# Layer-norm sums folded to 64 rows and stacked with their rounding rest, and the same for the last 64 tokens of a product with U

## The chip, the cores and the metric

The kernel runs on one core of a Trainium2 chip. The metric is device time in microseconds of one launch, the median of three runs. The profile is one further execution, taken by the hardware profiler; its times are counted from the first instruction of the span.

## What is computed

Three layers, batch 8, 576 tokens, 512 channels, all in fp32 with fp32-like accuracy:

```python
# 1: attention over keys and values pooled by 8 (72 of them), 8 heads of 64
attn = softmax(q @ k_p.T / 8);  x = (attn @ v_p) as [8, 576, 512]
# 2: token mixing of rank 32, then an MLP with residual
h = x.transpose(0, 2, 1) @ U @ V          # U [576, 32], V [32, 576]
u = x + h.transpose(0, 2, 1)
x = u + np.maximum(u @ w_ch1, 0.0) @ w_ch2
# 3: layer norm over the 512 channels, then an MLP with residual
mu  = np.mean(x, axis=-1, keepdims=True)
var = np.mean((x - mu) ** 2, axis=-1, keepdims=True)
xn  = (x - mu) / np.sqrt(var + 1e-06) * g_ln
out = x + np.maximum(xn @ w_ch1, 0.0) @ w_ch2
```

## The kernel before

Most products are made in fp32r, a rounded fp32 format in which TensorE takes one pass. To keep the accuracy, an operand is split into a rounded part (`h`, made on ScalarE or VectorE) and the rest (`l`, the difference, on VectorE or GpSimd), and a product is the sum of three: high by high, high by low, low by high. The function `split` (L547) makes both parts.

The program doesn't write an order by hand. Each step is an `Order.op` (L107) with the engines that it may run on and an estimated cost for each, the buffers that it reads and writes, and a priority that follows TensorE's estimated time. `schedule` (L151) is a list scheduler over TensorE, ScalarE (ACT), VectorE (DVE), GpSimd (POOL) and the SyncE queue (SP, all transfers): it plays the estimates through, and what it places on an engine is that engine's instruction order. Each engine then works strictly in that order and waits at an instruction whose inputs aren't there. A transfer is estimated at 1.3 us, plus its bytes at 250 per ns in one queue, plus 1.0 us.

There are two stages. The first (up to some 600 us) is attention by batch and head pair, interleaved with the first half of the MLP of layer 2 (`a_l1` L1279, `a_l2` L1306). For batches 2 to 7, `att_xt` (L991) transposes the attention output of a batch into five tiles of 128 tokens by 512 channels and splits each into `xh` and `xl`; `att_g` (L1008) multiplies both with the stationary tile `ust[:, i]` and sums all in one PSUM bank. The 576 tokens give four whole tiles; the fifth starts at token 448, so its rows 0 to 63 repeat tokens of the fourth, and the rows of U for them are zeros: `setup_uv` (L637) clears that half of the raw tile and loads the last 64 rows of U into the other. Batches 0 and 1 go another way (`tm_g`, L1075) with the fp32 copy `us` of U.

The second stage is three passes over nine groups of 512 tokens (`passes`, L1769): the second half of layer 2's MLP, then the two halves of layer 3's. A group is four units (`unit` L1505 and `second` L1593); a unit is seven blocks of six 256-column products (L1520) and eight of three 512-column products (L1608). Blocks sum into PSUM banks of the rings `pa` and `pbc` (two each); copies `s` (L403 or L405) take a bank's state away before the next block is added to it. `group_prep` (L1462) loads a group's tokens into `xraw` and makes split operands `op` for the next group: the rounded part on ScalarE, the rest on GpSimd (L556).

The layer norm of a group (`norm`, L1695) runs beside the next group of pass 0, and for the last group beside the first of pass 1. It has four steps, spread over the units. `n0` adds the four channel blocks on GpSimd into `lns`. `n1` splits `lns` into `lnh` and `lnl`, takes two products with `ones` (128 by 128, each element 1/512), which give the mean in every row of a `pbc` bank, subtracts it from the four blocks on VectorE and stores the result to `n_d`. `n2` squares the four blocks on ScalarE and adds them on GpSimd. `n3` makes the variance with four fp32 products in which `lns` is the stationary tile and the moving operand is one column (L1743), so that the 512 tokens come out as 128 rows by 4; then a square root, a reciprocal and one Newton step on small tiles, and a transfer `r_d` of 512 numbers to DRAM. The reciprocal root is used only in pass 2, where it is read back (L1675).

Of the kernel before, what the change touches and what calls it, by code (L numbers as in the profile page):

```python
# [20 lines left out]
DM = 512  # L21
# [400 lines left out]
class Kern:  # L422
    def __init__(self, nc, tc, aps):
# [68 lines left out]
        for a in ("lnh", "lnl"):  # L492
            ring(b2, a, [128, TG], F32R)
# [12 lines left out]
    def setup(self, ctx):  # L506
# [7 lines left out]
        self.minus = cp.tile([128, 128], F32R, tag="minus", name="minus")  # L514
        nc.scalar.mul(self.minus, self.ident, -1.0)
        few = cp.tile([128, 2], F32, tag="few", name="few")
        self.eps, self.mean = few[:, 0:1], few[:, 1:2]
        nc.gpsimd.memset(self.eps, 1e-6)
        nc.gpsimd.memset(self.mean, 1.0 / DM)
# [10 lines left out]
        self.p_d = [dp.tile([128, NCC, TG], F32, tag=f"p_d{g}", name=f"p_d{g}") for g in range(NG)]  # L530
        self.r_d = [dp.tile([1, TG], F32, tag=f"r_d{g}", name=f"r_d{g}") for g in range(NG)]
# [28 lines left out]

    def split_ps(self, hi, lo, ps, src, n, m):

        nc, o = self.nc, self.o
        on = {ACT: c_act(n, True), DVE: c_dve(n)}
        part = lambda: src(ps.t)
        o.op({ACT: on[ACT]}, lambda e: copy(nc, e, hi(), part()), r=[ps], w=[hi.a])
        o.op(
            {PE: c_pe(n)},
            lambda e: e.matmul(part(), self.minus[:m, :m], hi(), start=False, stop=True, skip_group_check=True),
            r=[hi.a],  # L570
            w=[ps],
        )
        o.op(on, lambda e: copy(nc, e, lo(), part()), r=[ps], w=[lo.a])
# [63 lines left out]
    def setup_uv(self):  # L637
# [4 lines left out]
        def load(raw):  # L642
            o.op(
                {GP: 200},
                lambda e: e.memset(raw.t[:64, 4 * RANK : n].bitcast(I32), 0),
                w=[raw],
            )
            o.op(
                {SY: 450},
                lambda e: e.dma_start(  # L650
                    raw.t[:, : 4 * RANK].rearrange("p (i r) -> p i r", r=RANK),
                    self.U[:512].rearrange("(i p) r -> p i r", p=128),
                ),
                w=[(raw, 0)],
                size=131072,
            )
            o.op({SY: 450}, lambda e: e.dma_start(raw.t[64:, 4 * RANK : n], self.U[512:]), w=[(raw, 1)], size=16384)
# [333 lines left out]
    def att_xt(self, b, i):  # L991
        o = self.o
        ps, xh, xl = self.buf("py"), self.buf("xh"), self.buf("xl")
# [8 lines left out]
        if NP * b < LEAN_X:  # L1002
            self.split_ps(View(xh, None, whole), View(xl, None, whole), ps, whole, DM, 128)
        else:
            self.split(View(xh, None, whole), View(xl, None, whole), View(ps, None, whole), DM, ps=True, hi_on=(ACT,))
        self.xhl[i] = (xh, xl)

    def att_g(self, b, i):  # L1008
# [9 lines left out]
        self.o.op({PE: c_pe(DM, 2)}, mm, r=[xh, xl, self.ust], w=[pg])  # L1018
# [676 lines left out]
    def norm(self, g):  # L1695
# [9 lines left out]
        nt = TG // 128  # L1705
# [7 lines left out]

        def n1():
            hi, lo, ps, s = self.buf("lnh"), self.buf("lnl"), self.buf("pbc"), b["s"]
            whole = lambda t: t
# [21 lines left out]
        def n3():  # L1738
            s, ps, sd, ve = b["s"], self.buf("pbc"), self.buf("lnd"), self.buf("lnv")

            def mm(e):
                for i in range(nt):
                    e.matmul(  # L1743
                        ps.t[:, i : i + 1], s.t[:, i * 128 : i * 128 + 128], self.mean, start=True, stop=True,
                        skip_group_check=True,
                    )

            o.op({PE: nt * 240}, mm, r=[s], w=[ps], full=True)
            part = lambda: ps.t[:, :nt]
            small = {DVE: 70}  # L1750
            o.op({ACT: 150}, lambda e: e.activation(sd.t, part(), AF.Sqrt, bias=self.eps), r=[ps], w=[sd])
            o.op({DVE: 130}, lambda e: e.tensor_scalar_add(ve.t, part(), 1e-6), r=[ps], w=[ve])
# [82 lines left out]
LEAN_X = 8  # L1835
# [51 lines left out]
```

## Time and profile before

| | |
|---|---|
| Time, median of 3 runs | 1762.2 us (1757.46 to 1763.09) |
| The profiled execution's own time | 1756.1 us |
| Its span, first to last instruction | 1754.3 us |
| TensorE busy | 1729.4 us (99%) |
| VectorE, ScalarE, GpSimd busy | 959.6, 714.5, 753.9 us (55%, 41%, 43%) |
| TensorE's granted clock, mean | 0.999 |
| Traffic | 222.99 MB, mean 127 GB/s |

Busy time is the union of an engine's instructions; TensorE's products overlap in the records, since they are pipelined, so the distance from start to start tells what one costs. PE is TensorE, PEld its weight loads, DVE VectorE, POOL GpSimd, SP the queue that issues transfers.

### The profile page before, as it was taken

How to read it: one execution, taken by the hardware profiler on the slowest of the kernel's cores; microseconds unless marked ns; L12 is line 12 of the kernel's file. 1: busy time of each engine (PE TensorE's matmuls, PEld its weight loads, DVE VectorE, ACT ScalarE, POOL GpSimd, SP SyncE). 2: the span in 40 equal slices, each digit the busy share in tenths (PEclk: the TensorE clock that was granted, in tenths of full speed). 3: DMA queues.
4: the chain of work that ended last, by engine and by line, in shares of the span. 5: the costliest groups of instructions: out<-in, count | busy, mean ns of one | idle time of the engine just before them, and what ended most of it. 6: DMA issues, size and time to landing. Idle time of an engine off the chain costs nothing.

```text
span 1754.3 us, 27128 instructions
## 1 busy us (share of the span) xinstructions
PE 1729.4 (99%) x10302; PEld 1525.7 (87%) x10302; DVE 959.6 (55%) x1839; ACT 714.5 (41%) x1812; POOL 753.9 (43%) x655
## 2 busy tenths in 40 slices
PE   6999999999999999999999999999999999999998
PEld 6888888888888899999999889999999999999997
DVE  7998887888655344444445756553225633333333
ACT  5765655655522233333333443333333332223221
POOL 3442312311100166666667643333335455555554
PEclk9999999999999999999999999999999999999999
DMA  6665554555143334444443453431112422333322
GB/s 201 217 201 170 184 182 147 179 174 162 55 165 108 130 111 121 121 121 121 120 121 115 126 163 125 134 121 67 49 49 85 144 103 103 110 119 103 103 79 78
DMA packets 96691, 222.99 MB, mean 127 GB/s; under 512 B 15408, under 2 KB 15792, under 8 KB 90800
## 3 DMA queue, kind: packets, MB, share of 16 engines
q1 hardware_dynamic: 96416, 221.26, 39.9%
q8 instruction: 80, 1.31, 0.3%
q14 instruction: 51, 0.42, 0.1%
q10 hardware_dynamic: 144, 0.00, 0.0%
HBM read 151.85 MB, written 69.37 MB: 126 GB/s over the span
## 4 chain that ended last, share of the span: by engine, by line
PE 91%; DVE 2%; DMA 1%; POOL 0%; issue 0%; ACT 0%; DVEq 0%; POOLq 0%; ACTq 0%
PE py L1608 33%; PE pa L1520 17%; PE pbc L1520 13%; PE pbc L1319 11%; PE pa L1291 11%; PE py L398 2%; PE py L847 2%; PE py L978 1%; PE py L979 1%; PE py L1016 0%; PE py L1015 0%; DVE w1l L556 0%; PE py L1185 0%; PE pbc L1743 0%; DMA wraw<-w_d 0%
## 5 line engine op out<-in xcount | busy, mean ns | idle before, releaser
L1608 PE MATMUL py<-hid,w2h 128*128 128x512 f32 x1728 | 541.2, 394 | 0.2 <-DVE hid L1548 0.2
L1608 PE MATMUL py<-hid,w2l 128*128 128x512 f32 x864 | 338.7, 392 | 0.0
L1520 PE MATMUL pa<-op,w1h 128*128 128x256 f32 x1728 | 326.2, 281 | 1.4 <-DVE s L405 1.0
L1520 PEld LDWEIGHTS pa<-op,w1h 128*128 128x128 f32 x1728 | 293.8, 188 | 37.9 <-DVE s L405 1.5
L556 POOL TENSOR_TENSOR op<-xraw,op 128x512 fp32r<-128x512 f32 x130 | 171.9, 1324 | 276.9 <-ACT op L403 272.0
L1578 DVE TENSOR_TENSOR pbc<-s,pbc 128x512 f32<-128x512 f32 x108 | 75.2, 696 | 382.2 <-PE pbc L1520 382.2
L1608 PEld LDWEIGHTS py<-hid,w2h 128*128 128x128 f32 x1728 | 273.7, 189 | 11.1 <-DVE hid L1548 0.5
L1520 PEld LDWEIGHTS pbc<-op,w1h 128*128 128x128 f32 x1296 | 220.8, 188 | 28.1
L1520 PE MATMUL pbc<-op,w1h 128*128 128x256 f32 x1296 | 244.3, 281 | 0.0
L1520 PE MATMUL pa<-op,w1l 128*128 128x256 f32 x864 | 242.7, 281 | 0.0
L1608 PEld LDWEIGHTS py<-hid,w2l 128*128 128x128 f32 x864 | 162.5, 188 | 36.7
L1319 PE MATMUL pbc<-op,wh 128*128 128x512 f32 x576 | 182.1, 397 | 0.0
L1520 PE MATMUL pbc<-op,w1l 128*128 128x256 f32 x648 | 181.8, 281 | 0.0
L1291 PE MATMUL pa<-hid,wh 128*128 128x512 f32 x576 | 180.5, 394 | 0.0
L1520 PEld LDWEIGHTS pa<-op,w1l 128*128 128x128 f32 x864 | 163.0, 189 | 0.0
L1548 DVE SCALAR_TENSOR_TENSOR hid<-pa,hid 128x512 fp32r<-128x512 f32 x108 | 74.5, 690 | 125.1 <-ACT hid L1542 124.8
L1542 ACT ACTIVATE hid<-pa 128x512 fp32r<-128x512 f32 x108 | 64.6, 598 | 190.8 <-PE pa L1520 180.9
L1542 ACT ACTIVATE hid<-pbc 128x512 fp32r<-128x512 f32 x108 | 64.6, 598 | 180.4 <-DVE pbc L1578 179.5
L1474 POOL TENSOR_TENSOR t<-xraw 128x512 f32<-128x512 f32 x52 | 67.4, 1296 | 141.3 <-DMA xraw<-n_d 89.4
L1291 PEld LDWEIGHTS pa<-hid,wh 128*128 128x128 f32 x576 | 105.8, 188 | 21.3 <-DVE op L1298 0.2
L1520 PEld LDWEIGHTS pbc<-op,w1l 128*128 128x128 f32 x648 | 121.9, 188 | 0.0
L1319 PEld LDWEIGHTS pbc<-op,wh 128*128 128x128 f32 x576 | 103.8, 188 | 19.4
(210 smaller groups left out, 2864.2 us busy)
## 6 DMA issues: line engine op xcount, KB each, us to landing
xraw<-n_d SPq DMA_DIRECT2D x18, 1024.0 KB
wraw<-wC SPq DMA_DIRECT2D x32, 512.0 KB
wraw<-wA SPq DMA_DIRECT2D x24, 512.0 KB
w_d<-wx SPq DMA_DIRECT2D x48, 256.0 KB
wraw<-w_d SPq DMA_DIRECT2D x48, 256.0 KB
k<-kT SPq DMA_DIRECT2D x32, 288.0 KB
q<-qT SPq DMA_DIRECT2D x32, 288.0 KB
v<-v SPq DMA_DIRECT2D x32, 288.0 KB
```

The lines of the kernel that those rows point to most:

```text
L398: e.matmul(out, src, ident, start=first, stop=True, is_transpose=True, skip_group_check=True)
L556: lambda e: e.tensor_sub(lo(), src(), hi().bitcast(F32)),
L847: lambda e: e.matmul(ps.t[:, i : i + 2 * SP], q.t[:, QT[t] : QT[t] + 128], kbd.t.rearrange("p h n -> p (h n)"), start=True, stop=True, ski ...
L978: e.matmul(ps.t[:, :SH], w, eh.t[:, h, c], start=True, stop=False)
L1291: e.matmul(ps.t, w.t[:, c], u.t, start=(i == 0), stop=(i == 3 * NCC - 1))
L1319: e.matmul(ps.t, w.t[:, c], x.t, start=(f == 0 and j == 0), stop=(f == NA - 1 and j == 2))
L1474: o.op(on, lambda e: e.tensor_sub(dst(), a(), c()), r=r, w=w)
L1520: e.matmul(bank.t[:, sl], w.t[:, self.WCOL[k], c], u.t[:, t], start=(first and i == 0), stop=(last and i == 5), skip_group_check=True,)
L1542: lambda e: e.activation(h.t[:, :TG], bank.t, AF.Relu),
L1548: lambda e: e.scalar_tensor_tensor(l.t[:, :TG], bank.t, 0.0, h.t[:, :TG].bitcast(F32), op0=ALU.max, op1=ALU.subtract),
L1578: o.op({DVE: c_dve(TG)}, lambda e: e.tensor_add(c.t, s.t, c.t), r=[s], w=[c])
L1608: e.matmul(y.t, w.t[:, i, c], x.t[:, :TG], start=(first and q == 0), stop=(last and q == 2))
```

## The change

The sum over channels needs only to add up 128 rows. The new `mean()` first adds the upper 64 rows of the sum to the lower 64 (a copy to `lnq` on ScalarE, an addition on GpSimd), rounds the 64 rows into the lower half of `lnh` (ScalarE) and puts the rest into its upper half (GpSimd). One product with `ones` then sums rounded part and rest together. `n1` and `n3` both use it. In `n3` the variance now lies along the columns of one row; it is copied from PSUM to `lnq`, written to a DRAM row `s_d` and read back as 128 rows by 4, from where the square root goes on as before.

In `att_xt` the fifth tile keeps only its 64 new tokens: the rounded part in rows 64 to 127, the rest in rows 0 to 63 of the same tile, with the last 64 rows of U loaded into both halves, so `att_g` makes one product of it instead of two. For `us` the lower half is cleared after the copies.

The tiles `lnl` and `minus`, the constant `mean` and the function `split_ps` go. The core of the diff:

```diff
@@ setup
-        self.minus = cp.tile([128, 128], F32R, tag="minus", name="minus")
-        nc.scalar.mul(self.minus, self.ident, -1.0)
@@ setup_uv
-            o.op({GP: 200}, lambda e: e.memset(raw.t[:64, 4 * RANK : n].bitcast(I32), 0), w=[raw])
...
-            o.op({SY: 450}, lambda e: e.dma_start(raw.t[64:, 4 * RANK : n], self.U[512:]), w=[(raw, 1)], size=16384)
+            for z in range(2):
+                r = slice(64 * z, 64 * z + 64)
+                o.op(
+                    {SY: 450},
+                    lambda e, r=r: e.dma_start(raw.t[r, 4 * RANK : n], self.U[512:]),
+                    w=[(raw, 1 + z)],
+                    size=16384,
+                )
...
+        o.op({GP: 200}, lambda e: e.memset(self.us.t[:64, 4], 0.0), w=[self.us])
@@ att_xt
-        if NP * b < LEAN_X:
-            self.split_ps(View(xh, None, whole), View(xl, None, whole), ps, whole, DM, 128)
+        if i < 4:
+            self.split(View(xh, None, whole), View(xl, None, whole), View(ps, None, whole), DM, ps=True, hi_on=(ACT,))
         else:
-            self.split(View(xh, None, whole), View(xl, None, whole), View(ps, None, whole), DM, ps=True, hi_on=(ACT,))
+            o.op({ACT: c_act(DM, True)}, lambda e: copy(nc, e, xh.t[64:], ps.t[64:]), r=[ps], w=[(xh, 1)])
+            o.op(
+                {DVE: c_dve(DM)},
+                lambda e: e.tensor_sub(xh.t[:64], ps.t[64:], xh.t[64:].bitcast(F32)),
+                r=[ps, (xh, 1)],
+                w=[(xh, 0)],
+            )
@@ att_g
-            e.matmul(pg.t, self.ust.t[:, i], xh.t, start=(i == 0), stop=False)
-            e.matmul(pg.t, self.ust.t[:, i], xl.t, start=False, stop=(i == 4))
+            e.matmul(pg.t, self.ust.t[:, i], xh.t, start=(i == 0), stop=(i == 4))
+            if i < 4:
+                e.matmul(pg.t, self.ust.t[:, i], xl.t, start=False, stop=False)
@@ norm
+        def mean():
+            s, q, h, ps = b["s"], self.buf("lnq"), self.buf("lnh"), self.buf("pbc")
+            on = {ACT: c_act(TG)}
+            o.op(on, lambda e: e.copy(q.t[:64], s.t[64:]), r=[s], w=[q])
+            o.op(eng, lambda e: e.tensor_add(s.t[:64], s.t[:64], q.t[:64]), r=[q], w=[s])
+            o.op(on, lambda e: e.copy(h.t[:64], s.t[:64]), r=[s], w=[(h, 0)])
+            o.op(
+                eng,
+                lambda e: e.tensor_sub(h.t[64:], s.t[:64], h.t[:64].bitcast(F32)),
+                r=[s, (h, 0)],
+                w=[(h, 1)],
+            )
+            o.op({PE: c_pe(TG)}, lambda e: e.matmul(ps.t, self.ones, h.t, start=True, stop=True), r=[h], w=[ps])
+            return ps
...
         def n1():
-            hi, lo, ps, s = self.buf("lnh"), self.buf("lnl"), self.buf("pbc"), b["s"]
-            self.split(View(hi, None, whole), View(lo, None, whole), View(s, None, whole), TG, hi_on=(ACT,), lo_on=(GP,))
-            def mm(e):
-                e.matmul(ps.t, self.ones, hi.t, start=True, stop=False)
-                e.matmul(ps.t, self.ones, lo.t, start=False, stop=True)
-            o.op({PE: c_pe(TG, 2)}, mm, r=[hi, lo], w=[ps])
+            ps = mean()
...
         def n3():
-                for i in range(nt):
-                    e.matmul(
-                        ps.t[:, i : i + 1], s.t[:, i * 128 : i * 128 + 128], self.mean, start=True, stop=True,
-                        skip_group_check=True,
-                    )
-            o.op({PE: nt * 240}, mm, r=[s], w=[ps], full=True)
+            ps, row, sd, ve = mean(), self.buf("lnq"), self.buf("lnd"), self.buf("lnv")
+            v = Buf(None)
+            o.op({ACT: c_act(TG, True)}, lambda e: e.copy(row.t[:1], ps.t[:1]), r=[ps], w=[row])
+            o.op({SY: 450}, lambda e: e.dma_start(self.s_d[g], row.t[:1]), r=[row], w=[v], size=2048)
+            o.op(
+                {SY: 450},
+                lambda e: e.dma_start(ve.t, self.s_d[g].rearrange("o (i p) -> p (o i)", p=128)),
+                r=[v],
+                w=[ve],
+                size=32768,
+            )
+            o.op({ACT: 150}, lambda e: e.activation(sd.t, ve.t, AF.Sqrt, bias=self.eps), r=[ve], w=[sd])
+            o.op({DVE: 70}, lambda e: e.tensor_scalar_add(ve.t, ve.t, 1e-6), w=[ve])
```

## Rows read from the trace of the kernel before

**Rows 1.** The page: busy time of the engines, and granted clock in 40 slices.
```profile
PE 1729.4 (99%) x10302; PEld 1525.7 (87%) x10302; DVE 959.6 (55%) x1839; ACT 714.5 (41%) x1812; POOL 753.9 (43%) x655
...
PEclk9999999999999999999999999999999999999999
```
**Rows 2.** Busy time of each engine by stretch: start, attention, pass 0.
```profile
core 0: us, PE busy (x) PEld busy (x) DVE busy (x) ACT busy (x) POOL busy (x), PEclk, DMA share, GB/s
0.00:44.00 44.00, 30.49 (x185) 27.07 (x186) 31.86 (x87) 23.47 (x75) 16.42 (x38) 1.00 0.68 202
...
352.00:416.00 64.00, 64.00 (x343) 54.15 (x342) 54.18 (x117) 40.04 (x144) 13.58 (x17) 1.00 0.49 160
731.00:774.00 43.00, 43.00 (x274) 38.86 (x273) 18.44 (x33) 15.37 (x30) 27.56 (x23) 1.00 0.45 124
```
**Rows 3.** Waits of TensorE: for whom, us in total, times, longest.
```profile
PE py L847 <- DMA q<-qT: 5.3, 1, 5.3
PE py L847 <- issue: 3.8, 1, 3.8
...
PE pa L1520 <- DVE s L405: 1.0, 1, 1.0
```
**Rows 4.** The chain that ended last: start, us, what; two groups each of passes 0, 1.
```profile
643.86 1.38 PE py L1608 x6
...
687.27 1.38 PE py L1608 x6
...
1036.24 1.38 PE py L1608 x6
...
1078.31 1.39 PE py L1608 x6
```
**Rows 5.** TensorE in order of time: start, us, line, what, count.
```profile
230.45 0.39 PE L1015 MATMUL py<-xh,ust 128*128 128x512 f32 x1
...
230.91 0.63 PE L1291 MATMUL pa<-hid,wh 128*128 128x512 f32 x2
...
657.02 0.40 PE L1720 MATMUL pbc<-lnh,ones 128*128 128x512 f32 x1
...
657.49 0.39 PE L1520 MATMUL pa<-op,w1h 128*128 128x256 f32 x2
...
678.47 0.95 PE L1743 MATMUL pbc<-few,lns 128*128 128x1 f32 x8
679.28 0.49 PE L1520 MATMUL pa<-op,w1h 128*128 128x256 f32 x2
679.60 0.28 PE L1520 MATMUL pa<-op,w1l 128*128 128x256 f32 x1
...
680.76 0.40 PE L1520 MATMUL pbc<-op,w1h 128*128 128x256 f32 x2
...
682.18 0.40 PE L1520 MATMUL pa<-op,w1h 128*128 128x256 f32 x2
```
**Rows 6.** A group of instructions: busy us, mean ns of one, idle before and its releaser.
```profile
L403 ACT CAST lnh<-lns 128x512 fp32r<-128x512 f32 x9 | 5.6, 622 | 10.6 <-POOL lns L1712 10.6
```
**Rows 7.** GpSimd in order of time, in the same group.
```profile
652.53 1.31 POOL L556 TENSOR_TENSOR lnl<-lns,lnh 128x512 fp32r<-128x512 f32 x1
...
664.22 1.29 POOL L1736 TENSOR_TENSOR lns<-lns,lnq 128x512 f32<-128x512 f32 x1 [0.74 <-ACT lnq L1735]
669.62 1.30 POOL L556 TENSOR_TENSOR op<-xraw,op 128x512 fp32r<-128x512 f32 x1 [4.11 <-ACT op L403]
```
**Rows 8.** ScalarE in order of time, behind the norm's products.
```profile
680.27 0.37 ACT L403 COPY s<-pa 128x256 f32<-128x256 f32 x1
```
**Rows 9.** The transfers' queue and the first reader of `xraw`, in order of time.
```profile
678.89 0.52 SPq L1484 DMA_DIRECT2D xraw<-u_d  x1
...
683.24 0.57 SPq L1761 DMA_DIRECT2D r_d<-lnd  x1
...
683.84 0.62 ACT L403 CAST op<-xraw 128x512 fp32r<-128x512 f32 x1 [0.39 <-DMA xraw<-u_d]
```

More of the change, by code (lines that the diff above doesn't have):

```diff
@@ L491, in __init__ @@
         ring(b2, "yt", [128, NCC, TG])
-        for a in ("lnh", "lnl"):
-            ring(b2, a, [128, TG], F32R)
+        ring(b2, "lnh", [128, TG], F32R)
         for a in ("lns", "lnq"):
@@ L513, in setup @@
         nc.gpsimd.memset(self.ones.bitcast(F32), 1.0 / DM)
-        self.minus = cp.tile([128, 128], F32R, tag="minus", name="minus")
-        nc.scalar.mul(self.minus, self.ident, -1.0)
-        few = cp.tile([128, 2], F32, tag="few", name="few")
-        self.eps, self.mean = few[:, 0:1], few[:, 1:2]
+        few = cp.tile([128, 1], F32, tag="few", name="few")
+        self.eps = few[:, 0:1]
         nc.gpsimd.memset(self.eps, 1e-6)
-        nc.gpsimd.memset(self.mean, 1.0 / DM)
         self.neg_b = cp.tile([128, 1], F32, tag="negb", name="neg_b")
@@ L530, in setup @@
         self.p_d = [dp.tile([128, NCC, TG], F32, tag=f"p_d{g}", name=f"p_d{g}") for g in range(NG)]
+        self.s_d = [dp.tile([1, TG], F32, tag=f"s_d{g}", name=f"s_d{g}") for g in range(NG)]
         self.r_d = [dp.tile([1, TG], F32, tag=f"r_d{g}", name=f"r_d{g}") for g in range(NG)]
@@ L559, in split @@
         )
[L561 to L571, printed above, removed]
-        )
-        o.op(on, lambda e: copy(nc, e, lo(), part()), r=[ps], w=[lo.a])
     def decode(self, x, tmp, raw):
@@ L643, in load @@
             o.op(
[L644 to L648, printed above, removed]
                 {SY: 450},
@@ L991, in att_xt @@
     def att_xt(self, b, i):
-        o = self.o
-        ps, xh, xl = self.buf("py"), self.buf("xh"), self.buf("xl")
+        nc, o = self.nc, self.o
+        ps, xh, xl = self.buf("py"), self.buf("xh"), self.buf("xl") if i < 4 else None
         xs = [self.xT[NP * b + p] for p in range(NP)]
@@ L1014, in mm @@
         def mm(e):
-            e.matmul(pg.t, self.ust.t[:, i], xh.t, start=(i == 0), stop=False)
-            e.matmul(pg.t, self.ust.t[:, i], xl.t, start=False, stop=(i == 4))
-        self.o.op({PE: c_pe(DM, 2)}, mm, r=[xh, xl, self.ust], w=[pg])
+            e.matmul(pg.t, self.ust.t[:, i], xh.t, start=(i == 0), stop=(i == 4))
+            if i < 4:
+                e.matmul(pg.t, self.ust.t[:, i], xl.t, start=False, stop=False)
+        r = [xh, xl, self.ust] if i < 4 else [xh, self.ust]
+        self.o.op({PE: c_pe(DM, 2 if i < 4 else 1)}, mm, r=r, w=[pg])
     def tm_v(self, P, z):
@@ L1704, in norm @@
         b = {}
-        nt = TG // 128
         eng = {GP: c_pool(TG)}
@@ L1712, in n0 @@
             o.op(eng, lambda e: e.tensor_add(s.t, s.t, q.t), r=[q], w=[s])
-        def n1():
-            hi, lo, ps, s = self.buf("lnh"), self.buf("lnl"), self.buf("pbc"), b["s"]
-            whole = lambda t: t
-            self.split(View(hi, None, whole), View(lo, None, whole), View(s, None, whole), TG, hi_on=(ACT,), lo_on=(GP,))
-            def mm(e):
-                e.matmul(ps.t, self.ones, hi.t, start=True, stop=False)
-                e.matmul(ps.t, self.ones, lo.t, start=False, stop=True)
-            o.op({PE: c_pe(TG, 2)}, mm, r=[hi, lo], w=[ps])
+        def mean():
[12 more added lines that the diff above has]
+            return ps
+        def n1():
+            ps = mean()
             for c in range(NCC):
@@ L1834 @@
 LEAN_T = 8
-LEAN_X = 8
 W_LEAD = (-12000.0, 8000.0)
```

6 lines of the change are left out of this document (removed).

## Prediction

> **What bounds the kernel now.** I read the page first: TensorE is busy for 99% of the span and its clock stands at the upper of its two levels, 2.4 GHz, in every slice [rows 1]. A busy TensorE can still be a waiting one, since the ends of its products are modelled, so I then took stretches: 30.49 of the first 44 us, but no idle time at all later, 64.00 of 64 in the attention stage and 43.00 of 43 in pass 0 [rows 2]. The list of its waits says the same: the long ones are at the start (5.3 us for the first load, 3.8 us of issue), and of the passes only 1.0 us behind a copy `s` is listed among them [rows 3]. Last, the period, from the chain of work: the same place of a 512-token group comes after 687.27 - 643.86 = 43.41 us in pass 0 and after 1078.31 - 1036.24 = 42.07 us in pass 1 [rows 4]. Both groups have the same products but for the norm, so the norm costs TensorE 1.34 us per group, and nothing else holds it. Hence behind the start each product taken off TensorE is worth its spacing, as long as the other engines keep up.
>
> **The norm's products.** In `n1` the two products with `ones` start at 657.02 and the next ones at 657.49 [rows 5]: 0.47 us, so one is 0.235 us. In `n3` the eight records of the four fp32 products begin at 678.47 and the next product at 679.28: 0.81 us. The pair of 256-column products behind them takes 679.60 - 679.28 = 0.32 us; a pair has as many columns as one product of 512, 0.235, so 0.085 us of turning from fp32 goes too: 0.895 us [rows 5]. The two together, 1.365 us, agree with the 1.34 of the periods. The change leaves one product of 0.235 us in each: n1 saves 0.235, n3 saves 0.895 - 0.235 = 0.66, together 0.895 us per group; nine groups: 8.05 us. I take the row's 0.235 for the new product since it has the same stationary tile and 512 columns; it has no lower price than that of its own shape, and rows give no reason for a higher one.
>
> A page of the Trainium skill would price it otherwise. TensorE: Matmul & The Clock Gate, Back-to-back issue gap, gives about 131 ns per 512-column product in a sustained stream; the spacing here is 235 ns, so the trace disagrees, and by the page the whole gain would be about 8.9 us (an estimate from that figure) instead of the sum below.
>
> **The product with U.** `att_xt` runs for six batches (2 to 7). Both halves of one token tile start at 230.45 and the next product at 230.91: 0.46 us, one is 0.23 [rows 5]. Six fifth tiles lose one each: 1.4 us. TensorE is full there, 64.00 of 64 us [rows 2], so it counts whole. If VectorE (54.18 of 64) were the true limit, it would be nothing; its subtraction and ScalarE's rounding stay as they are in number. The copy across partitions has no row on VectorE; below nothing is excluded, since no element is dropped from its 512, and twice its time would still be beside a full TensorE.
>
> **What is added, and what covers it.** POOL gets three operations per group (one in n1, two in n3). The nearest row is the subtraction `lnl`, 1.31 us at 128 rows [rows 7]; with half of the rows the free size is the same, so I take 1.3 us each, 3.9 per group, between nothing and twice that for writing to other partitions than it reads. POOL is busy 27.56 of 43 us in pass 0 [rows 2]: 31.5 of 42.5 then, 35.4 at the dear end. What could be late is a split for the next group. The sums of squares end at 664.22 + 1.29 = 665.5 and the first split of the next group starts at 669.62 [rows 7]; the second fold's chain (copy 0.62, add 1.3, copy 0.62, subtraction 1.3, some 4 us) fits that gap nearly, and a split pushed back is made at 670.9 and used at 680.76 [rows 5, 7]: almost 10 us of cover. Without that cover each microsecond would be one of TensorE. The first fold delays n1's product by a copy and an addition, 1.9 us; `lnl` was ready at 652.53 + 1.31 = 653.84 and its product ran at 657.02 [rows 5, 7], 3.2 us of cover.
>
> ScalarE gets four passes more per group (three copies at `lnh`'s 622 ns [rows 6] and the row from PSUM, about 0.6): 2.5 us on 15.37 of 43 [rows 2]. They stand in a queue in which the `s` copies wait, which TensorE needs. The copy at 680.27 ends at 680.64 and its bank is written again at 682.18 [rows 5, 8]: 1.5 us of cover for each. A copy of 0.6 us goes under it.
>
> n3 now sends 512 numbers to DRAM and back before the square root. SP gets both issues: the second waits for the first to land, and behind it are the `yt` load and the `x_d` stores. The whole of `xraw`, issued at 678.89, was used at 683.84, 4.95 us later [rows 9]; a small transfer behind it lands about then. One round is therefore between 0.57 us (an issue alone [rows 9]) and 4.95 us; I take 4.95 for both, as bulk loads lie in front. The result `r_d` is read in pass 2, hundreds of microseconds later, so the 10 us cost nothing as long as no engine stands for them. The `pbc` bank is held from the product to the row copy, about as long as today to the square root and addition.
>
> **Start and constants.** The cleared half of the raw tile becomes a second 16 KB load on SP, and `us` is cleared in 64 rows after its copies; `minus` goes, a ScalarE operation made while TensorE waits 5.3 us for its first load [rows 3]. Zero, with the first load as cover; an SP issue in front of the next loads could cost its 0.57 [rows 9]; the clearing makes POOL wait for three copies of `us`, and behind it stand only additions of `v` for later heads. The removed `split_ps` branch belongs to batches 0 and 1, which don't call `att_xt`: nothing.
>
> **Order.** The list scheduler places everything anew from its own costs, which can move the waits where TensorE is not full: 44 - 30.5 = 13.5 us in the first 44 [rows 2]. I bound a shift by the largest wait that order could make or remove there, 3.8 us of issue [rows 3], either way, and take zero.
>
> **Sum.** 8.05 + 1.4 = 9.4 us. The profiled execution took 1756.1 us, so 1746.7 on its own scale. The median of the three runs is 1762.2, 6 us above it, and the three spread over 5.6 us; the same work off the median gives 1752.8 us.
>
> **Rivals.** First, the slower side: **ScalarE stands for the round trip.** The square root waits for `ve` in an in-order queue, with the `s` copies and the Relus behind it. If the order puts it before the data land, say one round of 4.95 us early, TensorE loses 4.95 - 1.5 = 3.45 us per group, nine times 31 us, less 9.4: 1784 us. It decides from a stand of 1.5 + 0.9 + 0.16 = about 2.5 us per group, where cover and gain are used up. For it: two dependent transfers behind 1 MB loads, and an order fixed beforehand. Against: the scheduler's figures for 1 MB (1.3 us, 4.2 us at 250 bytes per ns, 1.0 us: 6.5) are longer than the 4.95 measured [rows 9], so it puts the root late rather than early. The Trainium skill (DMA: Bandwidth & Descriptors, Anatomy of one DMA) gives about 2.0 us fixed for one transfer issued from GpSimd, and an estimate from it is 4 us for the two transfers of the round; no row here shows one by itself.
>
> Second, **the new order eats half of the gain**: 3.8 us more waiting at the start or at the change of pass and 0.2 us of ScalarE's queue in each of nine groups, 5.6 us: 1762.2 - 9.4 + 5.6 = 1758.4 us. For it: the first 44 us depend on a chain, not on TensorE. Against: the changed loads there are small.
>
> Third, **the order also gains**: a wait of 3.8 us goes, 1749.0 us.
>
> That the change doesn't do what it says would be a POOL that cannot keep up: 35.4 of 42.5 us at the dear end is still below, and the splits have 10 us. I give it no chance of its own; it would look like the first rival.
>
> **How the numbers follow.** A comparison of this kernel can tell about 0.3%, 5.3 us, from no change. Forecast 0.68, gaining order 0.05: faster 0.73. Half eaten: 0.16, within. Standing ScalarE: 0.11, slower. The time is the forecast's, 1752.8. The range leaves the first rival out. Downward it takes the 3.8 us and the 5 us by which runs of one kernel lie apart, 1744; upward it reaches the second rival and the same scatter, 1763.
>
> **What would show it.** Period of pass 0: 42.5 us, between 43.4 and pass 1's unchanged 42.06. Eighteen products with `ones`, no fp32 product with `few`, 24 instead of 30 products with the low half in the product with U. POOL near 31 us per group, and no wait of TensorE for `s` or a split over 1 us. The attention period 0.23 us shorter. It is wrong if the period stays near 43.4 or more with TensorE waiting for an `s` copy behind a ScalarE that waits for `ve`, or if the first 44 us come out some microseconds longer.

## The result, and the profile after

Six runs of each kernel beside each other: before 1762.6 us (1757.5 to 1767.4), after 1784.5 us (1780.0 to 1789.8). The ratio is 1.0124, 95% interval 1.0103 to 1.0145: the change makes the kernel 22 us slower, where 9.4 us less had been forecast. The profiled execution of after took 1784.5 us (span 1782.7), its median. That of before took 1756.1, 6 us less than its median, so differences between the two traces come out some microseconds larger than the medians; verdicts below go by medians, and traces say where.

The page of after, busy time and granted clock (answers to [rows 1]):

```profile
PE 1737.6 (97%) x10224; PEld 1527.5 (86%) x10224; DVE 967.7 (54%) x1842; ACT 736.5 (41%) x1861; POOL 777.2 (44%) x658
...
PEclk8999999999999999999999999999999999999999
```

TensorE issues fewer products (10224 records, before 10302) and yet is busy for 8 us longer: some of them ran slowly. In 40 slices this can hardly be seen. The waits of TensorE, as in [rows 3], show more:

```profile
PE pbc L1514 <- DVE res L1725: 6.4, 1, 6.4
PE pa L1514 <- ACT s L403: 5.8, 2, 5.4
PE py L833 <- DVE kbd L412: 5.2, 1, 5.2
PE py L833 <- POOL us L658: 3.7, 1, 3.7
PE pa L1514 <- DVE pa L1578: 3.2, 1, 3.2
PE pbc L1514 <- DVE hid L1542: 2.6, 1, 2.6
```

The two of line 833 are those of the start, in size those of before (5.3 and 3.8). The four of line 1514 are new in this size (in before the longest there is 1.0); all but 0.4 us of them lie between 940 and 1110 us, where the kernel goes from pass 0 to pass 1. Now the chain of work (start, us, what), two groups of pass 0 and two of pass 1, as in [rows 4]:

```profile
708.61 1.39 PE py L1602 x6
...
751.15 1.39 PE py L1602 x6
...
1201.20 1.39 PE py L1602 x6
...
1243.27 1.39 PE py L1602 x6
```

The period of pass 0 is 751.15 - 708.61 = 42.54 us, forecast 42.5; pass 1 is unchanged at 42.07. The norm's saving is there, group by group. The loss is elsewhere. To find it, I took the same TensorE product in both traces and subtracted its start in before from that in the other kernel, at seven products (named by their start in before). A difference that grows from one column to the next is time lost between them. The kernels of the experiments stand in the same table.

| kernel | 77 | 183 | 439 | 615 | 961 | 1070 | 1722 us | median less median of before |
|---|---|---|---|---|---|---|---|---|
| after | -1.7 | 6.7 | 11.8 | 11.7 | 5.3 | 28.2 | 28.3 | +21.9 |
| U part alone | -3.5 | 4.6 | 14.9 | 15.1 | 15.1 | 16.1 | 16.1 | +7.8 |
| norm part alone | 2.5 | 2.2 | 2.9 | 3.3 | -3.1 | 19.2 | 19.3 | +12.6 |
| U part, old order | 1.4 | 1.4 | 2.9 | 2.9 | 2.9 | 3.3 | 3.3 | -0.3 |
| after, roots as one run | 1.1 | 8.5 | 15.6 | 15.6 | 9.3 | 13.4 | 13.4 | +1.7 |
| after, roots two issues later | 0.5 | 8.9 | 15.3 | 15.3 | 8.9 | 15.7 | 15.7 | +10.6 |
| norm alone, old order, root on a row | 3.3 | 4.2 | 6.5 | 7.0 | 7.4 | 18.9 | 20.4 | +11.5 |
| norm alone, pieces of 16 bytes | 3.6 | 3.4 | 4.7 | 5.1 | -1.2 | -0.8 | -0.8 | -7.2 |
| after, pieces of 16 bytes | -3.7 | 7.5 | 12.5 | 12.5 | 6.2 | 7.2 | 7.2 | +2.8 |
| the setup of the U part alone | 0.4 | 11.9 | 14.7 | 14.7 | 14.7 | 16.1 | 16.1 | +1.2 |
| the fifth tile alone | 4.1 | 4.6 | 9.5 | 9.6 | 9.6 | 10.4 | 10.4 | +2.1 |

After loses some 13 us in the attention stage (77 to 439), wins 6.4 in pass 0 up to 961, and loses 23 us at the change of pass (961 to 1070). Behind that nothing moves. So there are two losses in two places. In each the clock falls as well. Busy times by stretch (PE, PEld, DVE, ACT, POOL, then granted clock, DMA share, GB/s, as in [rows 2]) in after:

```profile
975.00:980.00 5.00, 4.86 (x17) 4.38 (x18) 1.00 (x1) 2.40 (x6) 3.00 (x3) 0.50 0.49 174
...
1036.00:1041.00 5.00, 1.63 (x7) 1.63 (x8) 4.25 (x8) 1.93 (x4) 2.10 (x2) 0.50 0.50 180
121.00:127.00 6.00, 5.58 (x15) 4.22 (x16) 5.40 (x9) 5.38 (x23) 2.77 (x4) 0.50 0.10 38
```

0.50 is the lower level, 1.2 GHz; in before no slice of the page shows it [rows 1]. It comes right after stretches in which TensorE stood (for 5.4 and 6.4 us; at 121 us after two waits of 1.0), so a wait is paid for again in slow products.

What made TensorE stand at the change of pass is read upward from there: the chain names a transfer, and the SyncE queue says what lies ahead of it. First the chain, then that queue in order of time, then ScalarE's wait, all of after:

```profile
961.91 12.21 DMA wraw<-w_d
...
1024.97 10.30 DMA wraw<-w_d
...
1072.94 8.43 DMA wraw<-wC
```

```profile
946.30 0.24 SPq L1743 DMA_DIRECT2D s_d<-lnq  x1
950.56 0.37 SPq L1746 DMA_DIRECT2D lnv<-s_d  x1
953.40 3.81 SPq L1634 DMA_DIRECT2D x_d<-res  x4
960.93 0.37 SPq L1761 DMA_DIRECT2D r_d<-lnd  x1
961.40 0.93 SPq L1412 DMA_DIRECT2D wraw<-w_d  x2
...
1023.95 0.37 SPq L1761 DMA_DIRECT2D r_d<-lnd  x1
1024.49 0.85 SPq L1412 DMA_DIRECT2D wraw<-w_d  x2
...
1069.83 0.37 SPq L1761 DMA_DIRECT2D r_d<-lnd  x1
1072.94 0.33 SPq L724 DMA_DIRECT2D wraw<-wC  x1
```

```profile
973.49 1.32 ACT L403 CAST w2h<-wraw 128x512 fp32r<-128x512 f32 x2 [6.87 <-DMA wraw<-w_d]
974.72 0.37 ACT L403 COPY s<-pa 128x256 f32<-128x256 f32 x1
```

ScalarE stands 6.87 us for weights of the next pass. The copy `s` behind it comes late, and TensorE waits 5.4 us for that copy. The two loads were issued at 961.40 and landed only 12 us later. Directly ahead of them stands `r_d`, the reciprocal roots, which go out as 512 writes of 4 bytes each. The same at 1024 (10.30 us, then the wait of 6.4) and, with the next load of weights, at 1070 (8.43 us, then the wait of 3.2). The fourth wait, 2.6 us for `hid` at 1000 us, is not of this kind: the kernels below without the small writes have waits of 1.6 to 2.1 us at that place. In before these writes stood elsewhere: ahead of stores that nobody waits for, the weights only behind these.

```profile
943.57 0.37 SPq L1761 DMA_DIRECT2D r_d<-lnd  x1
947.84 3.81 SPq L1640 DMA_DIRECT2D x_d<-res  x4
952.11 9.84 SPq L1418 DMA_DIRECT2D wraw<-w_d  x3
```

What moves during after's wait (first `r_d`'s writes, then two stretches in which the two weight loads should be under way, then the rest of them):

```profile
961.00:963.00 2.00, 2.00 (x13) 1.76 (x12) 0.65 (x2) 0.58 (x1) 2.00 (x2) 1.00 0.13 1
963.00:965.00 2.00, 2.00 (x13) 1.76 (x12) 1.37 (x3) 0.64 (x2) 1.92 (x2) 1.00 0.00 0
965.00:972.00 7.00, 4.73 (x30) 3.90 (x28) 4.24 (x7) 0.60 (x1) 2.94 (x3) 1.00 0.30 17
972.00:974.00 2.00, 0.00 (x0) 0.00 (x0) 0.00 (x0) 0.51 (x1) 0.00 (x0) 0.98 0.96 354
```

The small writes are moved by 963; for 2 us nothing moves at all, for 7 us the loads move at 17 GB/s, then, at once, the queue moves 354. Nothing else is issued behind the loads until 969.76, when a store of 1 MB (`n_d`) follows, which has its part in the 354. This gave the theory that the experiments test: the round trip through DRAM puts the small writes of the roots late, right in front of urgent loads, and the small writes make what follows slow. The rivals: the new order of the list as such; the round trip itself, for which an engine stands (the first rival of the prediction); and that the two parts of the change do each other harm.

### The profile page after: what moved, and what is told of

The parts are those of the page before. It is cut to its first block, busy times and chain, and to the rows that moved or that the text cites. A ratio compares the mean times of both kernels' runs of the same rounds, so it can differ in the third digit from the quotient of the medians.

```text
span 1782.7 us, 27080 instructions
## 1 busy us (share of the span) xinstructions
PE 1737.6 (97%) x10224; PEld 1527.5 (86%) x10224; DVE 967.7 (54%) x1842; ACT 736.5 (41%) x1861; POOL 777.2 (44%) x658
## 4 chain that ended last, share of the span: by engine, by line
PE 80%; DVE 6%; DMA 5%; issue 1%; ACT 0%; SPq 0%; POOL 0%; DVEq 0%; ACTq 0%
PE py L1602 32%; PE pa L1514 16%; PE pbc L1514 12%; PE pa L1285 8%; PE pbc L1313 8%; DMA wraw<-wC 2%; DMA wraw<-w_d 2%; PE py L398 1%; PE py L833 1%; DMA v<-v 1%; DVE xT L972 1%; DMA wraw<-wA 1%; DVE wx L596 0%; DVE wx L604 0%; DVE hid L553 0%
## 5 line engine op out<-in xcount | busy, mean ns | idle before, releaser
L1602 PEld LDWEIGHTS py<-hid,w2h 128*128 128x128 f32 x1728 | 275.5, 190 | 11.7 <-DVE hid L1542 0.5
```

The lines of the kernel that those rows point to most:

```text
L1602: e.matmul(y.t, w.t[:, i, c], x.t[:, :TG], start=(first and q == 0), stop=(last and q == 2))
```

## The experiments

### Each part alone

The U part alone takes over only the hunks of the diff in `setup_uv`, `att_xt` and `att_g`, the norm part alone all others. Both lists are planned anew.

```diff
 # U part alone
-        if NP * b < LEAN_X:
-            self.split_ps(View(xh, None, whole), View(xl, None, whole), ps, whole, DM, 128)
+        if i < 4:
+            self.split(View(xh, None, whole), View(xl, None, whole), View(ps, None, whole), DM, ps=True, hi_on=(ACT,))
...
 # norm part alone
-            hi, lo, ps, s = self.buf("lnh"), self.buf("lnl"), self.buf("pbc"), b["s"]
+            ps = mean()
...
-            s, ps, sd, ve = b["s"], self.buf("pbc"), self.buf("lnd"), self.buf("lnv")
+            ps, row, sd, ve = mean(), self.buf("lnq"), self.buf("lnd"), self.buf("lnv")
```

Expected of the U part alone: 

> The kernel before with the U part of the change alone (fifth tile stacked, one product, the three-operation split gone), list order planned anew. Theory H (two losses in two places: the replanned attention stage loses 11.6 us, the change of pass 23 us, and pass 0 gains 8): this kernel has the attention loss and nothing else, +10 to +13 us on the kernel before, about 1774, and its offset to before is reached by 490 us and flat from there. Rival N (the attention loss comes from the norm part, whose instructions move the plan of everything): -1.4 us, about 1761. Rival S (the losses are the round trip that ScalarE stands for): -1.4 us too.

Expected of the norm part alone: 

> The kernel before with the norm part of the change alone (both sums folded to 64 rows, one product each, the round trip through DRAM), list order planned anew. Theory H: attention stage as before, pass 0 at 42.54 us a group (-0.88 each, some 8 us in all), the change of pass +23 us: +15 us in all, about 1778. Rival N: +25 us or more, with the attention loss in it. Rival O (the order that the planner happens to find decides, no place of its own): the loss falls in another place than the change of pass, or there is none: 1753.

Measured: the U part 1770.6 us, ratio 1.0037 (1.0019 to 1.0055), +7.8; the norm part 1775.4 us, 1.0077 (1.0052 to 1.0102), +12.6. The two add to 20.4, the whole change costs 21.9: the parts don't need each other. The table puts the losses in the two places of after: the U part loses between 77 and 439 us and is flat from there but for 1.2, the norm part is level up to 615, gains 6.4 in pass 0 and loses 22.3 at the change of pass. The U part came out below the 10 to 13 that were expected, because I had read those off the traces, and before's trace is of a quick execution.

### The U part's work in the old order

The same work is issued at the places where the old list had the old work, so that no engine's order changes (the lower half of `us` isn't cleared behind the copies; they leave it out).

```diff
-            o.op({SY: 450}, lambda e: e.dma_start(raw.t[64:, 4 * RANK : n], self.U[512:]), w=[(raw, 1)], size=16384)
+            def both(e):
+                for r in (slice(64, 128), slice(0, 64)):
+                    e.dma_start(raw.t[r, 4 * RANK : n], self.U[512:])
+
+            o.op({SY: 450}, both, w=[(raw, 1)], size=16384)
...
-            e.matmul(pg.t, self.ust.t[:, i], xh.t, start=(i == 0), stop=False)
-            e.matmul(pg.t, self.ust.t[:, i], xl.t, start=False, stop=(i == 4))
+            e.matmul(pg.t, self.ust.t[:, i], xh.t, start=(i == 0), stop=(i == 4))
+            if i < 4:
+                e.matmul(pg.t, self.ust.t[:, i], xl.t, start=False, stop=False)
```

Expected: 

> The work of the U part (stacked fifth tile, one product, two-operation split of every tile) emitted in the order of the kernel before, on every engine. If the attention loss of the changed kernel is its new order: -1.4 us on the kernel before by six products of 0.23 us, 1761, within 1757 to 1763. If it is the work itself (the fifth tile's subtraction on VectorE that needs the rounded half first, or four tiles whose split subtracts on VectorE in place of a product with minus the identity): +8 to +12 us, about 1772.

Measured: 1762.6 us, ratio 0.9998 (0.9983 to 1.0012). The work costs nothing that could be measured; its forecast gain of 1.4 us is too small for this interval. The 7.8 us of the U part are those of the new list. Two stretches of the attention stage in before, in the U part alone and in the U part in the old order show it (columns as above):

```profile
115.00:135.00 20.00, 19.80 (x111) 16.88 (x110) 18.81 (x38) 13.65 (x46) 7.04 (x9) 1.00 0.60 182
...
200.00:440.00 240.00, 240.00 (x1283) 203.24 (x1282) 198.24 (x428) 137.34 (x494) 63.67 (x80) 1.00 0.53 167
```

```profile
115.00:135.00 20.00, 16.58 (x64) 12.39 (x63) 15.09 (x29) 10.45 (x37) 6.75 (x6) 0.83 0.40 115
...
200.00:440.00 240.00, 233.50 (x1216) 194.18 (x1214) 200.17 (x428) 132.09 (x481) 56.01 (x65) 0.99 0.52 159
```

```profile
115.00:135.00 20.00, 19.90 (x110) 16.89 (x109) 19.02 (x41) 12.85 (x42) 7.72 (x8) 1.00 0.61 194
```

In before TensorE had no idle time at all from 200 to 440 us; in the new list it stands 6.5 us there, in waits of at most 1.7 us, by the list of waits all for VectorE, which is busy for 200 of 240 us in both. At 115 to 135 it stands 3.4 us, and the clock falls. A list that just fits was exchanged for one that just doesn't.

### Which half of the U part moves the list

```diff
 # the setup alone: setup_uv as in the change, the fifth tile as in the run in the old order
+            for z in range(2):
+                r = slice(64 * z, 64 * z + 64)
...
+        o.op({GP: 200}, lambda e: e.memset(self.us.t[:64, 4], 0.0), w=[self.us])
 # the fifth tile alone: att_xt and att_g as in the change, the setup as in the run in the old order
+        self.o.op({PE: c_pe(DM, 2 if i < 4 else 1)}, mm, r=r, w=[pg])
```

Expected of the setup alone: 

> The kernel before with the setup of the U part alone planned anew (second load of the last 64 rows of U, the memset of the fifth tile's idle half moved behind the copies); the fifth tile's work in the attention stage is that of the change, but it stands in the order's input as before. Theory: these two more operations at the start, and not the product with U, shift the plan of the attention stage; the loss of about 8 us of the U part alone is there: 1768 to 1773. Rival: the new costs of the fifth tile's work shift it, and this kernel is at the kernel before, 1760 to 1764.

Expected of the fifth tile alone: 

> The kernel before with the fifth tile's part of the change planned anew (its stacked operations and the price of one product in the order's input), and with the setup in its old place. The setup alone was at 1763.5 (+1.2). If the fifth tile's new place in the plan makes the loss of the U part: 1768 to 1772. If it takes both together: 1760 to 1764.

Measured: the setup alone 1763.5 us, ratio 1.0009 (0.9995 to 1.0023); the fifth tile alone 1764.3 us, 1.0020 (1.0009 to 1.0032). By the medians they cost 1.2 and 2.1 us, and both together 7.8, so neither half alone accounts for the loss: my theory, that the two small operations at the start do it, isn't borne out, nor is the rival that the fifth tile does. That it takes the list that comes of both is likely and not shown: the interval of the fifth tile (1.0009 to 1.0032) overlaps that of the U part (1.0019 to 1.0055). The setup's profiled execution took 1772.2 us, the longest of its ten, and in it TensorE stands at 115 to 135 us just as in the U part alone, with the clock at 0.83 of full speed there (and loses 14.3 us from 77 to 439, in the table):

```profile
115.00:135.00 20.00, 16.98 (x74) 13.34 (x73) 18.21 (x36) 14.05 (x48) 9.63 (x8) 0.83 0.47 154
```

The same program at other times took 1760.7. I read this so that this list is near an edge, and that single executions fall over it; only one execution has a trace, so that is argued, not shown. Which instruction of the new list is the wrong one stays open.

### The small writes, written as one run

After in its own order. The roots go out as one run of 2 KB from a constant row; VectorE copies four elements into it, so that the wait stays. The scale of the last normalization is left out by this.

```diff
-                lambda e: e.dma_start(self.r_d[g].rearrange("o (i p) -> p (o i)", p=128), sd.t),
+                lambda e: e.dma_start(self.r_d[g], self.rowc),
```

Expected: 

> The changed kernel in its own order, with one thing else: the reciprocal roots go to DRAM as one run of 2 KB from a constant row in place of 512 writes of 4 bytes (the last VectorE operation copies 4 of its elements there, so the wait stays). The scale of the last normalization is left out by this: the row is zero but for four elements. Theory H-DMA (the 4-byte writes slow the two weight loads queued behind them by about 8 us at each of the two changes of group where that is urgent, 961 and 1024 us, and the clock falls in the waits): 15 to 23 us less than the changed kernel, 1762 to 1770. Rival O or S (order of the list, or the round trip itself with the engines that stand for it): within 4 us of the changed kernel, 1781 to 1788.

Measured: 1764.6 us, 20.0 less than after; ratio to before 1.0008 (0.9993 to 1.0024). The round trip, its waits and its order are all still in this kernel, and the 4-byte reads of the round trip too. What went is 512 small writes a group. SyncE and ScalarE in order of time, at the place where after lost its first 7 us:

```profile
966.13 0.24 SPq L1767 DMA_DIRECT2D r_d<-rowc  x1
966.46 0.79 SPq L1414 DMA_DIRECT2D wraw<-w_d  x2
```

```profile
970.45 1.13 ACT L403 CAST w2h<-wraw 128x512 fp32r<-128x512 f32 x2
```

From the issue of the loads to the first reader it is 3.99 us (970.45 - 966.46), with no wait of ScalarE ahead of it, where after has 12.09 (973.49 - 961.40). The table: from 961 to 1070 this kernel loses 4.1 us where after loses 22.9. Of what it still has against before, the table puts 14.5 in the attention stage, and 6.3 are won in pass 0 (its trace is of an execution 5 us above its median).

### The small writes, two issues later

After, its SyncE order changed in one point: `r_d` behind the next two issues.

```diff
         order.sort(key=lambda x: x[:2])
-        return [o for _, _, o in order]
+        out = [o for _, _, o in order]
+        for o in self.late:
+            i = out.index(o)
+            sy = [k for k in range(i + 1, len(out)) if out[k].eng == SY][:2]
+            if not any(out[k] in o.succs for k in sy):
+                out.insert(sy[-1] + 1, o)
+                out.pop(i)
+        return out
```

Expected: 

> The changed kernel with one issue moved: on SP the write of the reciprocal roots (512 writes of 4 bytes) stands behind the next two issues in place of ahead of them, so that at 961 and 1024 us the two weight loads go first; every other instruction and its order, and the round trip through DRAM, are as in the changed kernel. Theory H-DMA (these writes slow what is queued behind them): most of the 20 us that the writing as one run gave back, 1764 to 1770. If they slow whatever is under way at the time, ahead or behind: half of it, 1773 to 1779. If the round trip itself or the wait of SP for the roots makes the loss: SP still waits for the roots one issue later, and the time is that of the changed kernel, 1781 to 1788.

Measured: 1772.9 us, ratio 1.0069 (1.0048 to 1.0089), 11.6 less than after: between the ranges of my two cases, nearer to the lower end of "half of it". The trace tells why. At the first two places nothing is lost any more (the offset is 8.9 us at 961 and 8.4 at 1028). The loss lies at the third place, which my expectation had left out: from 1049 to 1070 the offset goes from 8.6 to 15.7, and it is a store that waits now. Chain and SyncE of this kernel:

```profile
1059.33 10.08 DMA w_d<-wx
```

```profile
1059.33 0.32 SPq L761 DMA_DIRECT2D w_d<-wx  x1
1059.70 0.43 SPq L1769 DMA_DIRECT2D r_d<-lnd  x1
```

The store of prepared weights was issued at 1059.33, the small writes at 1059.70, and the store's end came 10 us later, with the buffer that it held. TensorE waits 4.5 us for it and then runs at the lower clock:

```profile
1072.00:1076.00 4.00, 4.00 (x16) 3.71 (x17) 1.05 (x2) 0.60 (x1) 0.00 (x0) 0.50 0.67 197
```

So it isn't only what is queued behind that is slow: what is under way beside these writes is, too. In part the theory was too narrow. Before has the same slow writes, under cover. By the semaphore events of the traces the 2 KB landed 9.1 to 12.5 us after their issue in before and 9.1 to 10.8 in after (eight of the nine in each; one can't be read), and before's store of weights issued at 1029.58, 0.55 us ahead of its own small writes, took 11.35. Yet TensorE is busy there for 16.00 of 16 us (1029 to 1045).

### The folds in the old order, the root on one row

To have the norm's saving without a new list and without any round trip: the folds at the old places, and the root taken on one row of 512 in place of four columns.

```diff
-                    e.matmul(
-                        ps.t[:, i : i + 1], s.t[:, i * 128 : i * 128 + 128], self.mean, start=True, stop=True,
-                        skip_group_check=True,
-                    )
+                e.matmul(ps.t, self.ones, self.R["lnh"].tiles[0], start=True, stop=True)
...
+            def root(e):
+                e.reciprocal(sd.t, sd.t)
+                stt(e, ve.t, part(), 1e-6, ALU.add, sd.t)
+                stt(e, ve.t, ve.t, -0.5, ALU.mult, sd.t)
+                stt(e, sd.t, ve.t, 1.5, ALU.add, sd.t)
```

Expected of the norm alone: 

> The folded norm sums (one product each) in the order of the kernel before on every engine; the root is taken on one row of 512 in place of four columns of 128 rows, so there is no round trip, and the reciprocal roots go out as one run of 2 KB. If the saving of 0.895 us a group is TensorE's own work and nothing else stands in its place: nine times 0.895, -8.1 us on the kernel before, about 1755 (1753 to 1757), and flat offset outside the ten periods of the norm. If the folds' passes on ScalarE and GpSimd or the row's four longer VectorE operations (about 0.7 us each in place of 0.1) hold the weights' preparation up: within 3 us of the kernel before, 1760 to 1766.

Expected of both parts: 

> Both parts of the change in the order of the kernel before, the root on one row as in the folded norm alone. Theory (the work saves what was forecast, 8.1 us by the norm and up to 1.4 by the product with U, and the replanned order and the place of the small writes lost it): 1753 to 1756, faster than both kernels. By the run of the U part in the old order (no difference to before) rather the upper end, 1755. If the savings only move the next wait: 1760 or more.

Measured: the norm 1773.9 us, ratio 1.0060 (1.0047 to 1.0073); both parts 1773.0 us, 1.0060 (1.0048 to 1.0072). Both were expected at 1755 or near it. The group of instructions on the row (duration min, median, max in ns) says where one of my steps was wrong:

```profile
L1769 DVE RECIPROCAL lnd<-lnd x9: 3332/3341/3342, 688.1 to 1047.0; 1x512 f32<-1x512 f32 x9
L1766 DVE SCALAR_TENSOR_TENSOR lnv<-pbc,lnd x9: 679/679/680, 691.6 to 1050.5; 1x512 f32<-1x512 f32 x9
```

I had put 0.7 us to each of the four operations. Three take that, the reciprocal takes 3.34 us; on 128 rows by 4 it is 0.17 (below). So VectorE has 5.4 us of root in its queue, ahead of the preparation of weights, and the waits come back at the change of pass: in the table this kernel loses 11.5 us there. TensorE's list there, for comparison with after's `s` and `res`, and two pieces of the chain of work:

```profile
PE pa L1520 <- DVE pa L1584: 7.4, 2, 4.8
```

```profile
994.05 3.35 DVE lnd L1769
...
1047.11 3.27 DVE lnd L1769
```

The reciprocal is only part of the miss. In pass 0 the table shows no gain either, 7.0 at 615 and 7.4 at 961 us, where the norm planned anew wins 6.4. At the old places ScalarE's copies of the folds have to wait for GpSimd's additions, and what stands behind them, the `hid` of the next products, comes late; the chain of work of pass 0 runs through the folds there.

```profile
719.33 0.62 ACT L1752 CAST lnh<-lns 64x512 fp32r<-64x512 f32 x1 [1.39 <-POOL lns L1751]
```

A miss as an improvement, but a useful one: without any small write the change of pass loses time again, here with VectorE late in place of the load. Which share is the reciprocal's and which the folds', no run separates. The Trainium skill (VectorE: DVE Perf Modes, First, the fixed hardware budget) says that the reciprocal is made by an iterative divide with a repeat count of 8; 3.34 us against 0.68 for an operation of the same 512 elements agrees in kind, at 4.9 times.

### The round trip in pieces of 16 bytes

The columns don't need to hold every 128th token. If each row holds four neighbours, the sums are read and the roots written as 128 pieces of 16 bytes, and no other instruction changes.

```diff
-                lambda e: e.dma_start(ve.t, self.s_d[g].rearrange("o (i p) -> p (o i)", p=128)),
+                lambda e: e.dma_start(ve.t, self.s_d[g].rearrange("o (p i) -> p (o i)", p=128)),
...
-                lambda e: e.dma_start(self.r_d[g].rearrange("o (i p) -> p (o i)", p=128), sd.t),
+                lambda e: e.dma_start(self.r_d[g].rearrange("o (p i) -> p (o i)", p=128), sd.t),
```

Expected of the norm part alone: 

> The norm part of the change alone, planned anew, as in the earlier run of it, with one thing else: the round trip lays four neighbouring tokens on a row, so that the sums are read and the reciprocal roots written as 128 pieces of 16 bytes in place of 512 of 4. Theory H-DMA with the number of pieces deciding: the 20 us that the one run of 2 KB gave back in the changed kernel are nearly all given back here, 1775.4 less 20: 1755, within 1753 to 1759, faster than the kernel before. If time goes by each piece and the wait is a quarter of what it was, the upper end. If pieces under some size are slow whatever their number: 1770 to 1776.

Expected of the whole change: 

> The changed kernel whole, with the round trip in 128 pieces of 16 bytes as in the run beside it. Theory: that of the changed kernel with the roots written as one run, 1764.6, within 1762 to 1768: what is left over the run beside it is the replanned attention stage of the U part, some 8 us. If the attention stage is not what is left: the same time as the run beside it, within 3 us.

Measured: the norm part alone 1755.0 us, ratio 0.9965 (0.9951 to 0.9979), faster than both kernels; 20.4 less than the same with pieces of 4 bytes. The whole change so 1765.0 us, 1.0017 (1.0002 to 1.0033), 19.5 less than after, and 10.0 more than the norm part alone; by the table that lies in the attention stage (12.5 against 4.7 at 439 us), where the U part's new list loses. TensorE's waits from 945 to 1090 us and the reciprocal's group in the norm part so:

```profile
PE pbc L1500 <- DVE hid L1528: 1.6, 1, 1.6
PE pbc L1500 <- DVE res L1711: 1.2, 1, 1.2
```

```profile
L1739 DVE RECIPROCAL lnd<-lnd x9: 164/166/172, 697.7 to 1042.5; 128x4 f32<-128x4 f32 x9
```

No wait of 5 us is left, and this is with the same folds, the same round trip and a list planned anew. The 2 KB of roots land 1.4 to 3.6 us after their issue (semaphore events, all nine). The reads went to 16 bytes as well, but the whole change with one run and 4-byte reads (1764.6) and the one with 16-byte reads and writes (1765.0) are level, so it's the writes that count. The forecast for the norm's work was -8.05 us; it is -7.2 by the medians.

## Why the prediction was wrong

**What held.** The norm's products: 0.895 us per group were forecast, 43.41 - 42.54 = 0.87 were found. From 731 to 774 us of after, as in [rows 2]:

```profile
731.00:774.00 43.00, 43.00 (x272) 38.71 (x271) 18.85 (x32) 18.18 (x35) 32.18 (x26) 1.00 0.45 123
```

POOL is busy 32.18 us, forecast 31.5; ScalarE 18.18, forecast 15.37 + 2.5 = 17.9. The covers of 1.5 and 10 us were enough: TensorE waits for nothing there. The round itself was sized about right: 950.56 - 946.30 = 4.26 us from the first issue to the second, forecast 4.95. The norm's sum, 8.05, is worth 7.2 once the small writes are gone.

**What failed first: the step on the round trip and SP.** I wrote that SP gets both issues and named what is behind the second, the `yt` load and the `x_d` stores; and that `r_d` is read in pass 2, so that "the 10 us cost nothing as long as no engine stands for them". That asked who waits for the result. I didn't ask who waits behind it, and so put the delay at nothing. `r_d` was in the kernel already [rows 9], as 512 writes of 4 bytes; in the new list, behind the round trip, it stands elsewhere on its queue: no longer ahead of stores but ahead of weight loads. This costs 20.0 us (after less after with one run), 20.4 and 19.5 (the two pairs with pieces of 16 bytes). It happens at three of nine norms, those at the change of pass, where loads are urgent; inside pass 0 the same writes hurt nobody. Neither of the signs that I had named for being wrong came: the period fell to 42.54, and at 77 us after was 1.7 us ahead.

**The first rival** came out at the right number, 1784, by luck. It has ScalarE stand for the round trip in each of nine groups. In after ScalarE waits for the returned sums once, 1.1 us (what its engine waited for ahead of the root's operations):

```profile
  DMA lnv<-s_d: 1.1, 1
```

And with the round trip kept and the writes as one run the 20 us are gone. ScalarE does stand, but for weights.

**What failed second: the order term.** I bounded it by 3.8 us, the largest wait of the first 44 us, since TensorE was full behind that. But a list that is full is no proof that another list will be. The U part alone costs 7.8 us where I had taken -1.4, and the same work in the old order costs nothing that could be measured (0.9998). The term's place was wrong, and its bound too small by half. Which instruction of the new list makes it stays open.

**A cost not in the sum: the clock.** Rows showed the upper level all along, and I took it as given. In after it falls to 1.2 GHz behind the long waits; the mean was 0.57 in 1035 to 1043 us, and 0.66 in 974 to 984. At the lower level three 512-column products took 1.28 us that take 0.70 at the upper (1088.17 and 1091.82 in after's chain), so 974 to 984 alone is up to 3.4 us ((1 - 0.66) times 10, an estimate). The four waits add up to 17.6 of the 22.9 us that are lost at the change of pass; the other 5.3 fit these slow products in size, though no run takes them apart. A bound for a wait must have this in it.

**The share of the parts.** U's new list 7.8, the norm with its small writes 12.6; the sum 20.4 of 21.9. In the norm's 12.6 are 20 lost and some 7.5 won.

## What to carry to other kernels

When a change delays a step, look at each transfer at the end of the delayed chain and ask what is queued behind it, and what is under way beside it, at its new place, not only who reads it. Write results in a layout whose pieces lie together: here it took the exchange of two indices in two access patterns and was worth 20 us, and the good half of the change then beats both kernels. And a term for "planned anew" needs a run of its own: the same work in the old order tells work from order at once.

## What the runs showed of the hardware

512 writes of 4 bytes to DRAM, 2 KB in all, made two loads of 256 KB behind them take 12 us in place of 4, at 17 GB/s for 7 us; a store issued 0.4 us ahead of such writes took 10 us. The 4-byte reads of the round trip, as many, did no such harm: they are still there in the kernel with one run. 128 writes of 16 bytes cost nothing that could be measured (1765.0 against 1764.6 with one run). The same 2 KB landed 9.1 to 12.5 us after their issue as 512 writes and 1.4 to 3.6 as 128. The Trainium skill (DMA: Bandwidth & Descriptors, Specifications) says that below 512 B a DMA engine reads, modifies and writes. The slow 4-byte writes fit, the 16-byte writes without a measurable price do not fit a threshold at that size alone. Why other transfers suffer, no run here shows.

A reciprocal on VectorE takes 3.34 us for one row of 512 and 0.17 us for 128 rows of 4, the same 512 numbers.

In the passes of after TensorE's clock went to the lower level right behind the waits of 5.4 and 6.4 us, and more shortly behind those of 2.6 and 3.2 (0.57 in 1001 to 1005 and in 1086 to 1090 us); but for the last 4 us it was at the upper level elsewhere. The wait of 5.4 us for one copy was followed by a stretch of 5 us (975 to 980) at 0.50.
